# Gate of the first 32 units by Softplus and Erf in groups of three, in place of three Tanh and a Square

## The chip, the cores and the metric

The kernel runs on one core of one Trainium2 chip. Its time is the time on the device, in microseconds (us), of one execution; a number of executions are timed, and their median is given. Engines are named as in the profile: PE is TensorE's matmul, PEld its weight load, DVE is VectorE, ACT is ScalarE, POOL is GpSimd, SP is SyncE, which here issues most transfers.

## The reference

A small attention in two steps, then a feed-forward block with a gate. The gate is h * erf(softplus(h)).

```python
def sm_attn(qq, kk, vv):
    s = scale * np.matmul(qq, kk.transpose(0, 1, 3, 2))
    s = s - np.max(s, axis=-1, keepdims=True)
    a = np.exp(s)
    a = a / (np.sum(a, axis=-1, keepdims=True) + 1e-09)
    return np.matmul(a, vv)
p_packed = sm_attn(p, k, v)
out = sm_attn(q, p_packed, p_packed)
...
h = x @ w_in
sp = np.maximum(h, 0.0) + np.log1p(np.exp(-np.abs(h)))
g = h * erf(sp)
return (g @ w_out).astype(np.float32)
```

There are 8 batches of 8 heads, 576 positions and 64 numbers to a head; 32 packed queries p for each head. x is the attention's result, 4608 rows of 512; w_in is 512 x 2048 and w_out 2048 x 512. Both weights come as 64-bit floats.

## The kernel before

**Units.** The feed-forward part is cut into units. A unit (b, c, i) takes batch b, half c of its 576 positions (288 columns) and block i of eight blocks of 256 hidden features. `h_block` makes h for a unit in two PSUM tiles of 128 x 288 (12 matmuls, L264), copies them to one SBUF tile hs of 128 x 576 (L267, two passes on ACT, times 0.5) and applies the gate. `o_block` multiplies the gated tile with w_out and adds into four PSUM banks (L308). There are 128 units in a list. The first 32 are batches 0 and 1: first blocks 0 to 3 for the four pairs (b, c), 16 units, then blocks 4 to 7. This way only half the weights are needed at the start. The other 96 take batches 2 to 7 in turn, all eight blocks of one half after the other.

**The gate.** erf(softplus(h)) is not computed as written: it is approximated by three Tanh and a Square on ACT, with two weighted sums on DVE (L270 to L275), and a last product with hs. All these functions lie in the one activation table that is loaded at the start (L71), with Exp. In the first 12 units ("whole") the gated tile g goes to PE as it is in fp32. From unit 12 on it is split into a high and a low part (gh, gl, L286 and L287), and three matmuls in the faster fp32r type take the place of the fp32 one. h is always made from split operands.

**Attention.** `attention(b)` is a generator of 12 stages: loads of p and k, of v, of q; scores in two halves (L165); Exp of the first softmax (L174); transposes; the packed values pt (L198, L203); scores of the second step in two halves (L212, L215); Exp of the second softmax (L222); last its normalisation and the split of the result into a2h and a2l (L232, L233). `w_prime(b, j)` multiplies pt with a block of 512 features of w_in (L243) and splits the product (wph, wpl; L245, L246); this takes the place of forming x. h of batch b needs both a2 and these products.

**Weights.** A tile of the weights comes by DMA into a staging buffer (two of them, besides six places lent early by other tiles) and is turned from 64-bit to 32-bit by one pass on ACT (L87) and three on DVE (L88 to L90). 32 such tiles are needed; the last 24 are spread over the units by a plan. `split_w_out` splits w_out's tiles, from unit 14 on for the first half (L103, L104).

**What sets the order.** Loops emit the work unit by unit: h of unit n, then the planned items of unit n (`do(plan.pop(n, []))`: weights, stages of attention, w_prime, splits), then the out product of unit n - 3 (LAG). That order is a priority. A scheduler then gives each engine a fixed queue from it, by its own model of time. An engine works its queue in order, so an instruction that waits holds up all behind it on the same engine. ATT1 = (0, 2) spreads the 12 stages of batch 1's attention over the plan of units 0 to 2; batch 1's first unit is unit 8. Batch 2's stages lie at units 14 to 30, its first unit is unit 32. Pools: hs, t0 and t1 have three buffers each, gh and gl two each.

Of the kernel before, what the change touches and what calls it, by code (L numbers as in the profile page):

```python
# [8 lines left out]
F32 = mybir.dt.float32  # L9
F32R = mybir.dt.float32r  # L10
U32 = mybir.dt.uint32
I64 = mybir.dt.int64
AF = mybir.ActivationFunctionType
ALU = mybir.AluOpType
# [10 lines left out]
F64_SCALE = 2.0 ** -112  # L25
# [3 lines left out]
def tile_pack_attention_moe(ctx: ExitStack, tc: tile.TileContext, qT, kT, v, pT, w_in, w_out, outT):  # L29
    nc = tc.nc  # L30
    P = 128
    B, _, NC, S = qT.shape
    DFF = w_in.shape[1]
    DM = w_out.shape[1]
    HT = S // 2
# [3 lines left out]
    NBLK = DFF // (2 * P)  # L39
# [3 lines left out]
    NK = 32  # L43
    SCALE = 0.125
    LAG = 3
    NB0 = 2
    TURNS = (0, NBLK // 2, NBLK)
    WHOLE = 12
    SPLIT = 14
    WI_AT = (-1, 1)  # L50
    ATT1 = (0, 2)
    ATT2 = 14
    CONV = 2

# [7 lines left out]
    tpool = ctx.enter_context(tc.tile_pool(name="tmp", bufs=3))  # L62
# [5 lines left out]
    bias = cpool.tile([P, 4], F32, name="bias")  # L68
# [7 lines left out]
    def load_f32(dst, src, name, pool=None, tag="wst"):  # L76

        if src.dtype == F32:
            nc.sync.dma_start(dst, src)
            return  # L80
        n = src.shape[1]
        st = (pool or spool).tile([P, n], I64, name=name, tag=tag)
        nc.sync.dma_start(st[:], src)
        words = st[:].bitcast(U32).rearrange("p (n two) -> p n two", two=2)
        low, high = words[:, :, 0], words[:, :, 1]
        bits = dst.bitcast(U32)
        nc.scalar.activation(dst, high.bitcast(F32), AF.Abs, scale=F64_SCALE)  # L87
        nc.vector.tensor_scalar(bits, bits, 3, None, op0=ALU.logical_shift_left)  # L88
        nc.vector.scalar_tensor_tensor(bits, high, 0x80000000, bits, op0=ALU.bitwise_and, op1=ALU.bitwise_or)  # L89
        nc.vector.scalar_tensor_tensor(bits, low, 29, bits, op0=ALU.logical_shift_right, op1=ALU.bitwise_or)  # L90
# [9 lines left out]
    def split_w_out(f):  # L100
        hi = opool.tile([P, DM], F32R, name=f"woh{f}", tag="wo")
        lo = opool.tile([P, DM], F32R, name=f"wol{f}", tag="wo")
        nc.scalar.copy(hi[:], wo[f][:])  # L103
        nc.vector.tensor_tensor(lo[:], wo[f][:], hi[:], op=ALU.subtract)  # L104
        wo_hi[f], wo_lo[f] = hi, lo

    a2 = {}
    pt = {}
# [5 lines left out]
    def attention(b, roomy=False):  # L114
# [30 lines left out]
        k = [chunk(f"k{c}") for c in range(NC)]  # L145
# [5 lines left out]
        for j in range(NCH):  # L151
            n = min(P, S - j * P)
# [7 lines left out]
        a1 = apool.tile([P, 2, S], F32, name=f"a1_{b}", tag="big")  # L160
# [8 lines left out]
        m = apool.tile([P, 2], F32, name=f"m{b}", tag="m")  # L169
        nc.vector.tensor_reduce(m[:], a1[:], axis=AX.X, op=ALU.max)  # L170
        nc.vector.tensor_scalar(m[:], m[:], -SCALE, None, op0=ALU.mult)
        sm = apool.tile([P, 2], F32, name=f"sm{b}", tag="sm")
        for r in range(2):
            nc.scalar.activation(a1[:, r, :], a1[:, r, :], AF.Exp, bias=m[:, r:r + 1], scale=SCALE,  # L174
                                 accum_out=sm[:, r:r + 1])
        nc.vector.tensor_scalar(sm[:], sm[:], 1e-9, None, op0=ALU.add)
        nc.vector.reciprocal(sm[:], sm[:])
        for r in range(2):
# [15 lines left out]
        for j in range(NCH):  # L194
            n = min(P, S - j * P)
# [11 lines left out]
        ta = apool.tile([P, 2, S], F32, name=f"ta{b}", tag="big")  # L207
# [11 lines left out]
        wide = mx[:].unsqueeze(2).to_broadcast([P, 4 * nb, NK])  # L219
        nc.vector.tensor_reduce(mx[:], blocks, axis=AX.X, op=ALU.max)  # L220
        nc.vector.tensor_tensor(blocks, blocks, wide, op=ALU.subtract)
        nc.scalar.activation(ta[:], ta[:], AF.Exp, scale=SCALE)  # L222
        yield
        nc.vector.tensor_reduce(mx[:], blocks, axis=AX.X, op=ALU.add)
        nc.vector.tensor_scalar(mx[:], mx[:], 1e-9, None, op0=ALU.add)
# [21 lines left out]
        wp[b, j] = (hi, lo)  # L247

    gs = {}

    def h_block(b, c, i, whole):


        hs = tpool.tile([P, 2, HT], F32, name=f"hs{b}_{c}_{i}", tag="hs")
        for k in range(2):
            f = (2 * i + k) * P
            j, fo = f // FB, f % FB
            whi, wlo = wp[b, j]
            ps = ps_h.tile([P, 512], F32, name=f"h{b}_{c}_{i}_{k}", tag="ps_h")
            n = 0  # L260
            ahi, alo = a2[b]
            for r in range(2):
                for w, a in ((whi, ahi), (whi, alo), (wlo, ahi)):
                    nc.tensor.matmul(ps[:, 0:HT], w[:, r, fo:fo + P], a[:, r, c * HT:(c + 1) * HT],  # L264
                                     start=(n == 0), stop=(n == 5))
                    n += 1
            nc.scalar.mul(hs[:, k, :], ps[:, 0:HT], 0.5)  # L267
        t = tpool.tile([P, 2, HT], F32, name=f"t{b}_{c}_{i}", tag="t0")
        u = tpool.tile([P, 2, HT], F32, name=f"u{b}_{c}_{i}", tag="t1")
        nc.scalar.activation(t[:], hs[:], AF.Tanh, bias=bias[:, 0:1], scale=2.0 * T_SCALE)  # L270
        nc.scalar.activation(t[:], t[:], AF.Square, bias=bias[:, 1:2], scale=Q_SCALE)  # L271
        nc.scalar.activation(u[:], t[:], AF.Tanh, bias=bias[:, 2:3], scale=U_SCALE)  # L272
        nc.vector.scalar_tensor_tensor(t[:], t[:], 0.5 * A2, hs[:], op0=ALU.mult, op1=ALU.add)  # L273
        nc.vector.scalar_tensor_tensor(t[:], u[:], 0.5 * A1, t[:], op0=ALU.mult, op1=ALU.add)  # L274
        nc.scalar.activation(t[:], t[:], AF.Tanh, bias=bias[:, 3:4], scale=2.0 * A_SCALE)  # L275
        if whole:
            k = len(wholes) % 2
            wholes.append(i)
            g = tpool.tile([P, 2, HT], F32, name=f"g{b}_{c}_{i}", tag=("gh", "gl")[k], bufs=2)
            nc.vector.scalar_tensor_tensor(g[:], t[:], 1.0, hs[:], op0=ALU.add, op1=ALU.mult)  # L280
            gs[b, c, i] = (g,)
            return
        nc.vector.scalar_tensor_tensor(hs[:], t[:], 1.0, hs[:], op0=ALU.add, op1=ALU.mult)  # L283
        ghi = tpool.tile([P, 2, HT], F32R, name=f"gh{b}_{c}_{i}", tag="gh", bufs=2)
        glo = tpool.tile([P, 2, HT], F32R, name=f"gl{b}_{c}_{i}", tag="gl", bufs=2)
        nc.vector.tensor_copy(ghi[:], hs[:])  # L286
        nc.vector.tensor_tensor(glo[:], hs[:], ghi[:], op=ALU.subtract)  # L287
        gs[b, c, i] = (ghi, glo)

    wholes = []  # L290
    acc = {}
# [2 lines left out]
    def o_block(b, c, i, first, last):  # L294

        g = gs.pop((b, c, i))
        t0 = b * S + c * HT
        if first:
            acc[b, c] = []
            for d in range(NDM):  # L300
                po = ps_o.tile([P, 512], F32, name=f"o{b}_{c}_{i}_{d}", tag=f"ps_o{d}")
                acc[b, c].append(po)
        for d in range(NDM):
            for k in range(2):
                f = 2 * i + k
                terms = [(wo, g[0])] if len(g) == 1 else [(wo_hi, g[0]), (wo_hi, g[1]), (wo_lo, g[0])]
                for n, (w, gg) in enumerate(terms):
                    nc.tensor.matmul(acc[b, c][d][:, 0:HT], w[f][:, d * P:(d + 1) * P], gg[:, k, :],  # L308
                                     start=(first and k == 0 and n == 0),
                                     stop=(last and k == 1 and n == len(terms) - 1))  # L310
        if not last:
            return
        for d in range(NDM):
            ob = tpool.tile([P, HT], F32, name=f"ob{b}_{c}_{i}_{d}", tag="ob", bufs=NDM)
            nc.scalar.copy(ob[:], acc[b, c][d][:, 0:HT])
            where = outT[d * P:(d + 1) * P, t0:t0 + HT]
            if (b, c) in begun:
                nc.gpsimd.dma_start(where, ob[:], accum_op=ALU.add)
            else:
                nc.sync.dma_start(where, ob[:])  # L320
        begun.add((b, c))
# [4 lines left out]
    units = [(b, c, i, i == i0, i == i1 - 1) for b, c, i0, i1 in segs for i in range(i0, i1)]  # L326
# [50 lines left out]
    for k, (b, j) in enumerate(uses):  # L377
        if b not in ready:
            plan_attention(b)
        n = ready[b]  # L380
# [13 lines left out]
    def do(items):  # L394
        for it in items:
            if it[0] == "att":
                b = it[1]
                if b not in gens:
                    gens[b] = attention(b)
                next(gens[b])  # L400
            elif it[0] == "sp":
                split_w_out(it[1])
            elif it[0] in ("wi", "wo"):
                conversions[0] += 1
                slot = {}
                if 2 < conversions[0] <= 2 + len(EARLY):
                    slot = dict(pool=wpool, tag=EARLY[conversions[0] - 3])
                if it[0] == "wi":
                    load_w_in(it[1], it[2], **slot)
                else:  # L410
                    load_w_out(it[1], **slot)
            elif it[1:] == (0, 0):
                with tc.high_priority():
                    w_prime(0, 0)
            else:
                w_prime(it[1], it[2])
# [9 lines left out]
    for _ in range(STAGES - 3):  # L426
        next(first)
    do(early[4:])
    for n in range(len(units) + LAG):
        if n < len(units):  # L430
            h_block(*units[n][:3], n < WHOLE)
            do(plan.pop(n, []))
        if n >= LAG:
            o_block(*units[n - LAG])


# [36 lines left out]
```

## Time and profile before

| | us |
|---|---|
| median of 3 runs | 792.11 |
| lowest, highest | 791.83, 792.88 |
| the profiled execution, its own time | 789.89 |
| its span in the profile | 788.1 |

The profile follows one execution on the chip. Busy time is given for each engine, and idle time of an engine is put down to what ended it. A group of instructions has a line, an engine, an operation, its operands, the count, the busy time, the mean duration of one in ns and the idle time just before them. The page cuts the span into 40 slices of 19.7 us and gives the busy share of each in tenths; of these rows the ones of DVE, of ACT and of the clock that PE was granted (9 stands for nine tenths or more):

```profile
DVE  3887898977689678867887769767886769766664
ACT  3357778988689878887687868778687867878784
PEclk8568999999999999999999999999999999999999
```

The first 250 us are the first 13 digits: weights are turned there, two batches pass through attention, and the first 32 units are worked.

### The profile page before, as it was taken

How to read it: one execution, taken by the hardware profiler on the slowest of the kernel's cores; microseconds unless marked ns; L12 is line 12 of the kernel's file. 1: busy time of each engine (PE TensorE's matmuls, PEld its weight loads, DVE VectorE, ACT ScalarE, POOL GpSimd, SP SyncE). 2: the span in 40 equal slices, each digit the busy share in tenths (PEclk: the TensorE clock that was granted, in tenths of full speed). 3: DMA queues.
4: the chain of work that ended last, by engine and by line, in shares of the span. 5: the costliest groups of instructions: out<-in, count | busy, mean ns of one | idle time of the engine just before them, and what ended most of it. 6: DMA issues, size and time to landing. Idle time of an engine off the chain costs nothing.

```text
span 788.1 us, 15219 instructions
## 1 busy us (share of the span) xinstructions
PE 744.6 (94%) x6256; PEld 664.1 (84%) x6256; DVE 599.7 (76%) x916; ACT 597.6 (76%) x1011; POOL 15.1 (2%) x22
## 2 busy tenths in 40 slices
PE   3549988999999999999999999999999999999998
PEld 2228756899998898899799998889888998899998
DVE  3887898977689678867887769767886769766664
ACT  3357778988689878887687868778687867878784
POOL 0000000000111100000000000000000000000000
PEclk8568999999999999999999999999999999999999
DMA  8834735002542422013200222002300210000000
GB/s 306 291 110 149 243 116 162 31 17 67 107 88 31 83 76 89 1 39 98 80 32 1 83 81 72 13 1 80 132 32 1 79 47 1 31 2 31 1 31 31
DMA packets 31813, 58.39 MB, mean 74 GB/s; under 512 B 3584, under 2 KB 14848, under 8 KB 31744
## 3 DMA queue, kind: packets, MB, share of 16 engines
q1 hardware_dynamic: 29440, 55.06, 21.5%
q0 software_dynamic: 2304, 2.36, 2.6%
q8 instruction: 49, 0.80, 0.4%
q14 instruction: 20, 0.16, 0.1%
HBM read 45.61 MB, written 11.80 MB: 73 GB/s over the span
## 4 chain that ended last, share of the span: by engine, by line
PE 82%; DVE 7%; DMA 6%; ACT 3%; issue 1%; SPq 0%; ACTq 0%
PE o L308 50%; PE h L264 24%; PE wp L243 4%; DMA wi<-w_in 4%; DMA wos<-w_out 2%; PE p L198 2%; PE s L212 1%; PE s L165 1%; PE t L186 1%; DVE w_in_sb L89 1%; ACT t L270 1%; DVE wo L89 1%; ACT wo L87 1%; DVE w_in_sb L90 1%; DVE g L280 0%
## 5 line engine op out<-in xcount | busy, mean ns | idle before, releaser
L308 PE MATMUL o<-gl,woh 128*128 128x288 f32 x928 | 273.3, 295 | 0.0
L308 PE MATMUL o<-gh,woh 128*128 128x288 f32 x928 | 273.1, 300 | 0.0
L308 PE MATMUL o<-gh,wol 128*128 128x288 f32 x928 | 272.9, 295 | 0.0
L308 PEld LDWEIGHTS o<-gh,woh 128*128 128x128 f32 x928 | 172.1, 187 | 25.5 <-DVE t L273 8.9
L308 PEld LDWEIGHTS o<-gl,woh 128*128 128x128 f32 x928 | 174.3, 188 | 1.8 <-issue 1.3
L308 PEld LDWEIGHTS o<-gh,wol 128*128 128x128 f32 x928 | 174.6, 188 | 1.5 <-issue 1.3
L267 ACT ACTIVATE hs<-h 128x288 f32<-128x288 f32 x256 | 103.2, 412 | 95.4 <-PE h L264 94.6
L264 PE MATMUL h<-a2h,wph 128*128 128x288 f32 x512 | 155.2, 304 | 10.6 <-ACT wph L245 5.9
L264 PE MATMUL h<-a2l,wph 128*128 128x288 f32 x512 | 152.7, 298 | 1.8 <-DVE a2l L233 1.8
L264 PE MATMUL h<-a2h,wpl 128*128 128x288 f32 x512 | 152.6, 298 | 0.0
L283 DVE SCALAR_TENSOR_TENSOR hs<-t,hs 128x576 f32<-128x576 f32 x116 | 87.7, 756 | 72.5 <-ACT t L275 72.5
L275 ACT ACTIVATE t<-t,bias 128x576 f32<-128x576 f32 x128 | 98.8, 772 | 25.3 <-DVE t L274 25.0
L264 PEld LDWEIGHTS h<-a2h,wph 128*128 128x128 f32 x512 | 97.2, 190 | 22.3 <-ACT wph L245 6.8
L273 DVE SCALAR_TENSOR_TENSOR t<-t,hs 128x576 f32<-128x576 f32 x128 | 95.9, 750 | 20.1 <-ACT u L272 19.8
L270 ACT ACTIVATE t<-hs,bias 128x576 f32<-128x576 f32 x128 | 99.6, 778 | 2.9
L271 ACT ACTIVATE t<-t,bias 128x576 f32<-128x576 f32 x128 | 99.3, 775 | 2.3
L264 PEld LDWEIGHTS h<-a2l,wph 128*128 128x128 f32 x512 | 97.4, 190 | 4.3 <-DVE a2l L233 2.8
L272 ACT ACTIVATE u<-t,bias 128x576 f32<-128x576 f32 x128 | 99.3, 776 | 1.8
L264 PEld LDWEIGHTS h<-a2h,wpl 128*128 128x128 f32 x512 | 97.3, 190 | 1.9 <-issue 1.9
L274 DVE SCALAR_TENSOR_TENSOR t<-u,t 128x576 f32<-128x576 f32 x128 | 96.3, 752 | 1.6
L287 DVE TENSOR_TENSOR gl<-hs,gh 128x576 fp32r<-128x576 f32 x116 | 87.3, 753 | 1.5
L286 DVE CAST gh<-hs 128x576 fp32r<-128x576 f32 x116 | 52.9, 456 | 35.0 <-PE o L308 33.8
(60 smaller groups left out, 637.3 us busy)
## 6 DMA issues: line engine op xcount, KB each, us to landing
k<-kT SPq DMA_DIRECT2D x32, 288.0 KB, 4.3
q<-qT SPq DMA_DIRECT2D x32, 288.0 KB, 4.3
outT<-ob SPq DMA_DIRECT2D x64, 144.0 KB, 1.8
wi<-w_in SPq DMA_DIRECT2D x16, 512.0 KB, 6.0
v<-v SPq DMA_DIRECT2D x32, 256.0 KB, 3.6
wos<-w_out SPq DMA_DIRECT2D x16, 512.0 KB, 3.6
outT<-ob POOLq DMA_DIRECT2D x16, 144.0 KB, 3.7
v<-v SPq DMA_DIRECT2D x8, 128.0 KB, 4.2
```

Of the source, the lines that this page charges most:

```text
L264: nc.tensor.matmul(ps[:, 0:HT], w[:, r, fo:fo + P], a[:, r, c * HT:(c + 1) * HT], start=(n == 0), stop=(n == 5))
L267: nc.scalar.mul(hs[:, k, :], ps[:, 0:HT], 0.5)
L270: nc.scalar.activation(t[:], hs[:], AF.Tanh, bias=bias[:, 0:1], scale=2.0 * T_SCALE)
L271: nc.scalar.activation(t[:], t[:], AF.Square, bias=bias[:, 1:2], scale=Q_SCALE)
L272: nc.scalar.activation(u[:], t[:], AF.Tanh, bias=bias[:, 2:3], scale=U_SCALE)
L273: nc.vector.scalar_tensor_tensor(t[:], t[:], 0.5 * A2, hs[:], op0=ALU.mult, op1=ALU.add)
L274: nc.vector.scalar_tensor_tensor(t[:], u[:], 0.5 * A1, t[:], op0=ALU.mult, op1=ALU.add)
L275: nc.scalar.activation(t[:], t[:], AF.Tanh, bias=bias[:, 3:4], scale=2.0 * A_SCALE)
L283: nc.vector.scalar_tensor_tensor(hs[:], t[:], 1.0, hs[:], op0=ALU.add, op1=ALU.mult)
L286: nc.vector.tensor_copy(ghi[:], hs[:])
L287: nc.vector.tensor_tensor(glo[:], hs[:], ghi[:], op=ALU.subtract)
L308: nc.tensor.matmul(acc[b, c][d][:, 0:HT], w[f][:, d * P:(d + 1) * P], gg[:, k, :], start=(first and k == 0 and n == 0), stop=(last and k = ...
```

## The change

In the first 32 units (GROUPED) the gate is now computed as written: Softplus, Erf and a product. Softplus and Erf are done for three units at a time: three Softplus, then three Erf, then the products (and splits) of the three. 32 units make ten groups of three and one of two. A chain of dependencies without a wait (`in_turn`) fixes the order of Softplus, Erf and attention's Exp on ACT while units 0 to 31 are emitted. hs is no longer halved in these units, and its buffers alternate between the tags hs and t1 from group to group. Out products run 5 units behind while n < 32 (LAG_G), then 3 as before. The stages of batch 1's attention are spread over units 1 to 6. The pass on ACT that turns weights is a multiplication in place of Abs. From unit 32 on the gate is as it was.

```diff
+    G = 3
+    GROUPED = 4 * NBLK
+    LAG_G = 5
...
-    ATT1 = (0, 2)
+    ATT1 = (1, 6)
...
-        nc.scalar.activation(dst, high.bitcast(F32), AF.Abs, scale=F64_SCALE)
+        nc.scalar.mul(dst, high.bitcast(F32), F64_SCALE)
...
+    functions = []
+    grouping = [True]
+
+    def in_turn(ins):
+
+        if grouping[0] and functions:
+            tc.add_manual_dep(ins.ins, functions[-1], mybir.DependencyInfo(
+                mybir.DependencyClass.NoSync, mybir.DependencyReason.DATA), reason="table")
+        functions.append(ins.ins.name)
...
-            nc.scalar.activation(a1[:, r, :], a1[:, r, :], AF.Exp, bias=m[:, r:r + 1], scale=SCALE,
-                                 accum_out=sm[:, r:r + 1])
+            in_turn(nc.scalar.activation(a1[:, r, :], a1[:, r, :], AF.Exp, bias=m[:, r:r + 1], scale=SCALE,
+                                         accum_out=sm[:, r:r + 1]))
...
-        nc.scalar.activation(ta[:], ta[:], AF.Exp, scale=SCALE)
+        in_turn(nc.scalar.activation(ta[:], ta[:], AF.Exp, scale=SCALE))
...
+    group = []
...
+    def gate_group():
+
+        ts = []
+        for hs, b, c, i, whole in group:
+            t = tpool.tile([P, 2, HT], F32, name=f"t{b}_{c}_{i}", tag="t0")
+            in_turn(nc.scalar.activation(t[:], hs[:], AF.Softplus))
+            ts.append(t)
+        for t in ts:
+            in_turn(nc.scalar.activation(t[:], t[:], AF.Erf))
+        for t, (hs, b, c, i, whole) in zip(ts, group):
+            if whole:
+                nc.vector.tensor_tensor(whole_g(b, c, i)[:], t[:], hs[:], op=ALU.mult)
+            else:
+                nc.vector.tensor_tensor(hs[:], t[:], hs[:], op=ALU.mult)
+                split_g(hs, b, c, i)
+        group.clear()
...
+        grouped = n < GROUPED
+        hs = tpool.tile([P, 2, HT], F32, name=f"hs{b}_{c}_{i}", tag="t1" if grouped and n // G % 2 else "hs")
...
-            nc.scalar.mul(hs[:, k, :], ps[:, 0:HT], 0.5)
+            if grouped:
+                nc.scalar.copy(hs[:, k, :], ps[:, 0:HT])
+            else:
+                nc.scalar.mul(hs[:, k, :], ps[:, 0:HT], 0.5)
+        if grouped:
+            group.append((hs, b, c, i, whole))
+            if len(group) == G or n == GROUPED - 1:
+                gate_group()
+            return
...
+    behind = 0
     for n in range(len(units) + LAG):
         if n < len(units):
-            h_block(*units[n][:3], n < WHOLE)
+            grouping[0] = n < GROUPED
+            h_block(*units[n][:3], n < WHOLE, n)
             do(plan.pop(n, []))
-        if n >= LAG:
-            o_block(*units[n - LAG])
+        while behind <= n - (LAG_G if n < GROUPED else LAG):
+            o_block(*units[behind])
+            behind += 1
```

`whole_g` and `split_g` hold the lines that made g, or gh and gl, in `h_block` before.

More of the change, by code (lines that the diff above doesn't have):

```diff
@@ L249, in tile_pack_attention_moe, with split_g, whole_g, h_block @@
     gs = {}
-    def h_block(b, c, i, whole):
-        hs = tpool.tile([P, 2, HT], F32, name=f"hs{b}_{c}_{i}", tag="hs")
+    group = []
+    def split_g(hs, b, c, i):
+        ghi = tpool.tile([P, 2, HT], F32R, name=f"gh{b}_{c}_{i}", tag="gh", bufs=2)
+        glo = tpool.tile([P, 2, HT], F32R, name=f"gl{b}_{c}_{i}", tag="gl", bufs=2)
+        nc.vector.tensor_copy(ghi[:], hs[:])
+        nc.vector.tensor_tensor(glo[:], hs[:], ghi[:], op=ALU.subtract)
+        gs[b, c, i] = (ghi, glo)
+    def whole_g(b, c, i):
+        k = len(wholes) % 2
+        wholes.append(i)
+        g = tpool.tile([P, 2, HT], F32, name=f"g{b}_{c}_{i}", tag=("gh", "gl")[k], bufs=2)
+        gs[b, c, i] = (g,)
+        return g
+    def gate_group():
[13 more added lines that the diff above has]
+        group.clear()
+    def h_block(b, c, i, whole, n):
+        grouped = n < GROUPED
+        hs = tpool.tile([P, 2, HT], F32, name=f"hs{b}_{c}_{i}", tag="t1" if grouped and n // G % 2 else "hs")
         for k in range(2):
@@ L259, in h_block @@
             ps = ps_h.tile([P, 512], F32, name=f"h{b}_{c}_{i}_{k}", tag="ps_h")
-            n = 0
+            m = 0
             ahi, alo = a2[b]
@@ L264, in h_block @@
                     nc.tensor.matmul(ps[:, 0:HT], w[:, r, fo:fo + P], a[:, r, c * HT:(c + 1) * HT],
-                                     start=(n == 0), stop=(n == 5))
-                    n += 1
-            nc.scalar.mul(hs[:, k, :], ps[:, 0:HT], 0.5)
+                                     start=(m == 0), stop=(m == 5))
+                    m += 1
+            if grouped:
[7 more added lines that the diff above has]
+            return
         t = tpool.tile([P, 2, HT], F32, name=f"t{b}_{c}_{i}", tag="t0")
@@ L276, in h_block @@
         if whole:
[L277 to L281, printed above, removed]
+            nc.vector.scalar_tensor_tensor(whole_g(b, c, i)[:], t[:], 1.0, hs[:], op0=ALU.add, op1=ALU.mult)
             return
         nc.vector.scalar_tensor_tensor(hs[:], t[:], 1.0, hs[:], op0=ALU.add, op1=ALU.mult)
[L284 to L288, printed above, removed]
+        split_g(hs, b, c, i)
     wholes = []
```

## The prediction

> **What bounds the kernel now.** I read the page first (engines, then the 40 slices), then who TensorE (PE) waited for, then the stretches between 80 and 140 us, then the lines of time around the longest waits.
>
> ```profile
> span 788.1 us, 15219 instructions
> PE 744.6 (94%) x6256; PEld 664.1 (84%) x6256; DVE 599.7 (76%) x916; ACT 597.6 (76%) x1011; POOL 15.1 (2%) x22
> ...
> PE   3549988999999999999999999999999999999998
> ```
>
> PE is the bound from about the seventh slice on. Its busy time is modelled, so I use only its waits and the order of its groups. Who PE waited for between 46 and 160 us (us in total, times, longest):
>
> ```profile
> PE h L264 <- ACT wph L245: 5.9, 1, 5.9
> PE wp L243 <- DVE wpl L246: 2.3, 2, 1.8
> PE wp L243 <- DVE w_in_sb L90: 1.9, 2, 1.4
> PE h L264 <- DVE a2l L233: 1.8, 1, 1.8
> PE o L308 <- DVE g L280: 1.8, 2, 1.2
> PE t L186 <- DVE wpl L246: 1.0, 1, 1.0
> PE h L264 <- ACT hs L267: 0.5, 2, 0.3
> ```
>
> Together 15.2 us. The same view from 160 us to the end has its heading and no row. How far the units with the changed gate reach is seen from the product at L273, one for each unit, between 46 and 245 us (DVE busy, count, clock, DMA share, GB/s):
>
> ```profile
> 46.00:245.00 199.00, 23.29 (x31) 0.96 0.38 108
> ```
>
> So units 0 to 31 fill 46 to about 245 us, and the 96 units behind them, where PE never waits, keep their code. Whatever the change saves on ACT and DVE, it can win at most these 15.2 us and what the waits hide. The stretches (busy us of PE, PEld, DVE, ACT, POOL, then granted clock, DMA share, GB/s):
>
> ```profile
> 80.00:100.00 20.00, 19.91 (x131) 14.18 (x130) 17.12 (x29) 16.28 (x30) 0.00 (x0) 1.00 0.74 251
> 100.00:120.00 20.00, 16.49 (x85) 10.80 (x84) 20.00 (x30) 14.00 (x21) 0.00 (x0) 0.91 0.32 99
> 120.00:140.00 20.00, 17.42 (x114) 12.61 (x114) 16.15 (x27) 17.98 (x34) 0.00 (x0) 1.00 0.46 146
> 140.00:160.00 20.00, 20.00 (x126) 16.73 (x125) 18.41 (x28) 18.71 (x36) 0.00 (x0) 1.00 0.09 31
> ```
>
> From 100 to 120 DVE is busy all the time and PE starves. What it starves of is attention of batch 1, which unit 8 needs (lines of time; start, us):
>
> ```profile
> 55.35 0.76 ACT L174 ACTIVATE a<-a,m 128x576 f32<-128x576 f32 x1
> ...
> 57.72 0.99 ACT L245 CAST wph<-wp 128x1024 fp32r<-128x1024 f32 x1
> ```
>
> ```profile
> 116.38 1.34 DVE L233 TENSOR_TENSOR a2l<-tb,a2h 128x1152 fp32r<-128x1152 f32 x1
> ```
>
> ```profile
> 46.34 0.61 PE L264 MATMUL h<-a2l,wph 128*128 128x288 f32 x1 [1.81 <-DVE a2l L233]
> ...
> 78.57 4.04 PE L308 MATMUL o<-g,wo 128*128 128x288 f32 x16
> ...
> 106.94 5.84 PE L308 MATMUL o<-g,wo 128*128 128x288 f32 x16
> ...
> 115.58 4.15 PE L308 MATMUL o<-g,wo 128*128 128x288 f32 x16 [1.17 <-DVE g L280]
> 119.35 0.64 PE L264 MATMUL h<-a2h,wph 128*128 128x288 f32 x2
> ```
>
> Batch 1's first Exp starts at 55.35, its last split ends at 117.7, and h of unit 8 starts at 119.35. Ahead of it PE has done the out products of units 0 to 7, the last two at 106.94 and 115.58.
>
> **The change, part by part.** The groups that carry prices (busy us, mean ns; idle before):
>
> ```profile
> L267 ACT ACTIVATE hs<-h 128x288 f32<-128x288 f32 x256 | 103.2, 412 | 95.4 <-PE h L264 94.6
> L270 ACT ACTIVATE t<-hs,bias 128x576 f32<-128x576 f32 x128 | 99.6, 778 | 2.9
> L275 ACT ACTIVATE t<-t,bias 128x576 f32<-128x576 f32 x128 | 98.8, 772 | 25.3 <-DVE t L274 25.0
> L273 DVE SCALAR_TENSOR_TENSOR t<-t,hs 128x576 f32<-128x576 f32 x128 | 95.9, 750 | 20.1 <-ACT u L272 19.8
> L274 DVE SCALAR_TENSOR_TENSOR t<-u,t 128x576 f32<-128x576 f32 x128 | 96.3, 752 | 1.6
> L280 DVE SCALAR_TENSOR_TENSOR g<-t,hs 128x576 f32<-128x576 f32 x12 | 9.0, 749 | 0.2 <-ACT t L275 0.2
> L222 ACT ACTIVATE ta<-ta 128x1152 f32<-128x1152 f32 x8 | 9.3, 1166 | 9.0 <-DVE ta L221 8.9
> L246 DVE TENSOR_TENSOR wpl<-wp,wph 128x1024 fp32r<-128x1024 f32 x32 | 38.9, 1216 | 6.1 <-ACT wph L245 5.0
> L138 ACT COPY a<-s 128x576 f32<-128x576 f32 x14 | 8.8, 626 | 1.8 <-PE s L165 1.7
> L71 ACT ACT_TABLE_LOAD x1 | 1.3, 1283 | 0.7 <-PEq L465 0.7
> ```
>
> 1. *DVE.* L273 and L274 go, and the product at L280/L283 becomes a plain product of the same size (taken at 750). Per unit 0.750+0.752 = 1.50 us less, 48 us over 32 units.
>
> 2. *ACT functions.* Four passes of about 775 become two without a bias tile. The trace has neither Softplus nor Erf. The passes without a bias tile are 626 (a copy of 576) and 1166 (Exp of 1152); from 412 at 288 to 1166 at 1152 a line gives 0.66 at 576. I take 0.67, ends 0.626 and 0.778. The edits from mul 0.5 to copy and from Abs to mul are one pass for one pass: nothing, also in their waits.
>
> 3. *Table loads.* The trace has one, 1283 ns. Taking it that Softplus, Erf and Exp each need their own table (the diff strings them together with the reason "table"), 32 units are 11 groups with 2 loads each, the two Exp places of batch 1 and the two of batch 2 fall between groups and add 4, the return to Exp and Tanh adds 1: 27 more. I take 1.28 us each, as the row nearest to it is the thing itself; its ends are 0 where it runs while ACT waits for data anyway, and twice the row, 2.57, if the engine also empties around it. So ACT for three whole units was 6 x 0.412 + 12 x 0.775 = 11.8 us and becomes 6 x 0.412 + 6 x 0.67 + 2 x 1.28 = 9.1 (11.6 by the upper end). PE needs about three times 1.6 + 4.04 = 17 us for the same three units (h: 12 matmuls in 1.60 us; out product: the row at 78.57):
>
> ```profile
> 144.19 1.60 PE h L264 x12
> ```
>
> So ACT stays under PE in the steady part. The Trainium skill, "ScalarE: Activation LUTs", section "What ACT_TABLE_LOAD costs", puts a switch at 1283 ns plus a drain of about 1380 ns, 2.66 us in all; the trace agrees with the first part and cannot show the second, its only load standing ahead of all work. By that page three units would take 6 x 0.412 + 6 x 0.67 + 2 x 2.66 = 11.8 us, an estimate, so ACT would win nothing.
>
> 4. *Lag 5.* Between h of the last unit of a group and the first out product of that group PE has three h and three out products, 14 to 17 us. The gate chain of a group after that h is an eviction, one Softplus, a load, an Erf and one DVE product: 0.41+0.67+1.28+0.67+0.75 = 3.8 us, plus what stands ahead in the queues. I count no wait in the steady part. The two buffers each of gh and gl make the third unit of a group wait for its first one's out product, which is done a whole unit ahead of the third one's: nothing, as long as PE runs. At unit 32 three out products are caught up, the same work as before.
>
> 5. *The wait that is added.* Erf of units 6 and 7 stands behind Softplus of unit 8 on ACT, and unit 8 needs batch 1. So out products 6 and 7, which now fill PE until 119.35, can run only after it. Queued behind: PE has nothing but six out products ahead of h of unit 8.
>
> 6. *Batch 1 is moved.* Its stages go from units 0 to 2 to units 1 to 6, so its loads go behind the second block of w_in and the first two of w_out on SP's queue (a gain for those, a loss for k; both hidden, as its scores run while PE waits for that w_in block's product anyway). Its first Exp now stands behind Erf of unit 2. Unit 2 needs the split whose cast starts at 57.72; with batch 1's Exps and a tanh gone from ahead of it I take it 2 us earlier, then split, h, eviction, Softplus, load, three Erf and load: 1.0+1.2+1.6+0.4+0.7+1.3+2.0+1.3 = 9.5, so Exp at about 65 instead of 55.35.
>
> *The sum.* Let T be the end of batch 1's last split (before: 117.7). From 46.34 to 119.35 are 73.0 us, with waits of 15.2 less 1.8 (a2l, at its start) and less 2.6 that come after 119.35 (1.4 of w_in_sb, 0.5 of hs, 0.6 of g): 10.8. The out product at 106.94 took 5.84 where 4.04 is usual, so 1.8 more are hidden. Work: 73.0-10.8-1.8 = 60.4, less out products 6 and 7 (8.1): 52.3. PE would be through with it at 98.6; then it waits until T. Allowing 1.0 for later waits in place of 2.6, the change is (T-98.6+1.0) - (10.8+1.8+2.6) = T - 112.8. For T: the chain from first Exp to last split took 62.4 us in a DVE queue that is nearly full. Removed from that queue are 8 units x 2.25 = 18 us, put in 6 units x 0.75 = 4.5: 13.5 less. 65+62.4-13.5 = 113.9. A queue no longer full also costs each chain step less; I take 5 us for that, about a third of the removed work, by choice. T = 109, change **-3.8 us**. The ends: T at or below 98.6 gives -14.2; T with no relief at all, 127, gives +15. The profiled execution ran 789.89 us for a span of 788.1; 786.1 after it. The median of the runs shown is 2.2 us higher, so 788.3 on that scale.
>
> **The rivals.**
> - *A, forecast, 0.40*: as above, 781 to 790.5.
> - *B, the waits nearly vanish, 0.20*: batch 1 is ready by 101.5. For: only short DVE ops stand between its steps then. Against: its first Exp is 10 us later. 792.1-14 to -11: 778 to 781.
> - *C, the new wait takes the place, 0.19*: out products 6 and 7 held behind batch 1 (part 5) cost 8 us of PE, and DVE's relief is used up by weight conversions that move forward. It decides from T = 114.4 on; at T = 120, +7: 799, range 793.7 to 802.
> - *D, the switches cost twice the row, 0.08*: 27 x 1.28 = 35 us more on ACT, which from 120 to 160 us is busy 36.7 of 40. ACT then wins nothing, and two switches and the Erf ahead lengthen the chain by some 4 us: T about 117, +4, 796. More loads than 27 (the order not kept) would look the same. The Trainium skill, "ScalarE: Activation LUTs", section "What ACT_TABLE_LOAD costs", states a rule of this kind, a drain with every switch.
> - *E, no difference, 0.13*: the start is paced by the weights (transfer, ACT, DVE, two staging buffers), as the chain of waits has it:
>
> ```profile
> 84.89 3.50 DMA wos<-w_out
> 90.44 3.80 DMA wos<-w_out
> 118.96 3.92 DMA wi<-w_in
> ```
>
> Then relief on DVE changes little: 790.5 to 793.7.
>
> **How the numbers follow.** A measurement of this kernel tells about 0.2% (1.6 us) from no change. Faster: A+B = 0.60; same: E = 0.13; slower: C+D = 0.27. Range 778 to 799: it leaves out the upper part of C, about 0.1, and little below B, and its ends are those that T (the sum) and the load (part 3) give. The likeliest sign's own range is 778 to 790.5.
>
> **What would show it.** Right: DVE under 17 of 20 between 100 and 120 us; 28 loads of about 1.3 us; h of unit 8 before 112; waits of PE up to 138 us near 12 in sum and none behind. Wrong: a wait of PE on a g or on hs after 140 us (part 4), loads with an idle ACT of over 1 us behind them (part 3), h of unit 8 at 119 or later with PE idle before it (part 5), or Exp of batch 1 at 70 or later (part 6).

## The result and the profile after

The changed kernel takes 819.79 us (median of 4 runs, 819.15 to 820.72) against 792.39 before: the ratio is 1.0347, interval 1.0329 to 1.0365. It is 27 us slower, outside the predicted range. The profiled execution ran 820.72 us for a span of 818.9. The page after, engines and three rows of the slices:

```profile
span 818.9 us, 15125 instructions
PE 749.7 (92%) x6256; PEld 664.5 (81%) x6256; DVE 560.9 (68%) x852; ACT 583.0 (71%) x974; POOL 15.0 (2%) x22
...
PE   3359844999999999999999999999999999999998
...
DVE  3886668343438567977697678867797778776664
...
PEclk8569965999999999999999999999999999999999
```

In both kernels PE is at nine tenths or more from the eighth digit to the last but one, though DVE is busy 39 us less than before. The sixth and seventh digits (about 100 to 140 us), which were 8, are now 4: PE idle, and with a lowered clock. The stretches of that time (busy us of PE, PEld, DVE, ACT, POOL; clock, DMA share, GB/s):

```profile
100.00:120.00 20.00, 10.60 (x124) 5.99 (x120) 13.56 (x24) 3.97 (x8) 0.00 (x0) 0.74 0.79 258
120.00:140.00 20.00, 6.88 (x45) 2.91 (x45) 16.21 (x22) 13.22 (x18) 0.00 (x0) 0.57 0.16 53
140.00:160.00 20.00, 19.87 (x111) 13.81 (x112) 6.11 (x9) 15.70 (x27) 0.00 (x0) 0.91 0.09 30
```

From 100 to 120 us DVE is no longer full (13.56 for 20.00), ACT almost idle, and the transfers run at 258 GB/s. None of the compute engines is full. Who PE waited for after 46 us; these rows come to 33.1, and to 38.3 with six smaller ones that are not shown, where it was 15.2:

```profile
PE wp L256 <- DVE wpl L259: 11.2, 2, 10.8
PE s L225 <- DVE ta L228: 4.2, 1, 4.2
PE o L354 <- DVE g L290: 4.2, 2, 2.4
PE h L310 <- ACT wph L258: 4.0, 1, 4.0
PE h L310 <- ACT a2h L245: 3.5, 1, 3.5
PE h L310 <- ACT hs L314: 3.0, 2, 2.0
PE h L310 <- DVE a2l L246: 3.0, 1, 3.0
```

So 23 of the 31 us between the two spans are waits of PE after 46 us. 2.4 more are waits before it (27.4 for 25.0). What is left, 5 us, is PE working longer on the same 6256 matmuls (749.7 for 744.6 us busy), at a lower clock. The product with w_in behind the longest wait takes 1.96 us, where the one at 105.86 took 1.09 in the kernel before:

```profile
127.19 1.96 PE L256 MATMUL wp<-w_in_sb,pt 64*32 64x512 f32 x16 [10.81 <-DVE wpl L259]
```

What PE waits for is batch 1. Lines of time of ACT, up to its first Exp:

```profile
66.04 0.62 ACT L151 COPY a<-s 128x576 f32<-128x576 f32 x1
...
73.23 0.67 ACT L90 ACTIVATE wo<-wos 128x512 f32<-128x512 f32 x1 [4.82 <-DMA wos<-w_out]
73.81 0.62 ACT L151 COPY a<-s 128x576 f32<-128x576 f32 x1
...
77.95 1.28 ACT L187 ACT_TABLE_LOAD   x1 [0.33 <-DVE m L184]
79.25 0.78 ACT L187 ACTIVATE a<-a,m 128x576 f32<-128x576 f32 x1
```

and up to its second:

```profile
108.19 0.66 ACT L90 ACTIVATE w_in_sb<-wi 128x512 f32<-128x512 f32 x1 [5.38 <-DMA wi<-w_in]
110.94 0.66 ACT L90 ACTIVATE w_in_sb<-wi 128x512 f32<-128x512 f32 x1 [2.09 <-DMA wi<-w_in]
114.29 0.68 ACT L90 ACTIVATE wo<-wos 128x512 f32<-128x512 f32 x1 [2.69 <-DMA wos<-w_out]
119.28 0.66 ACT L90 ACTIVATE wo<-wos 128x512 f32<-128x512 f32 x1 [4.30 <-DMA wos<-w_out]
119.95 1.28 ACT L235 ACT_TABLE_LOAD   x1
121.25 1.16 ACT L235 ACTIVATE ta<-ta 128x1152 f32<-128x1152 f32 x1
```

The first Exp comes at 79.25 in place of 55.35, and each step stands in ACT's queue behind passes over weights whose transfers have not landed. On DVE, the data of the second Exp was ready at 118.56; ACT was held by the weights until 119.94. The longest wait of PE, 10.8 us, ends the same way: the split that it waits for needs a cast, and the product to be cast was there at 116.4, but the cast stood in ACT's queue behind the last of these weights, the Exp, two Softplus and two loads:

```profile
124.88 0.99 ACT L258 CAST wph<-wp 128x1024 fp32r<-128x1024 f32 x1
```

The last split of batch 1:

```profile
133.80 1.35 DVE L246 TENSOR_TENSOR a2l<-tb,a2h 128x1152 fp32r<-128x1152 f32 x1
```

It ends at 135.15 (T of the prediction), 17 us later than before.

### The profile page after: what moved, and what is told of

The parts are those of the page before. It is cut to its first block, busy times and chain, and to the rows that moved or that the text cites. A ratio compares the mean times of both kernels' runs of the same rounds, so it can differ in the third digit from the quotient of the medians.

```text
span 818.9 us, 15125 instructions
## 1 busy us (share of the span) xinstructions
PE 749.7 (92%) x6256; PEld 664.5 (81%) x6256; DVE 560.9 (68%) x852; ACT 583.0 (71%) x974; POOL 15.0 (2%) x22
## 4 chain that ended last, share of the span: by engine, by line
PE 80%; DMA 7%; ACT 6%; DVE 5%; issue 1%; SPq 1%; ACTq 0%
PE o L354 49%; PE h L310 23%; PE wp L256 4%; DMA wi<-w_in 4%; PE p L211 2%; DMA q<-qT 1%; PE s L225 1%; DMA wos<-w_out 1%; PE s L178 1%; PE t L199 1%; DVE wo L92 1%; ACT L287 1%; ACT t L287 1%; ACT w_in_sb L90 1%; ACT t L284 1%
## 5 line engine op out<-in xcount | busy, mean ns | idle before, releaser
L310 PE MATMUL h<-a2h,wph 128*128 128x288 f32 x512 | 157.3, 308 | 20.4 <-ACT a2h L245 13.4
L316 ACT ACTIVATE hs<-h 128x288 f32<-128x288 f32 x192 | 78.2, 412 | 80.4 <-PE h L310 77.3
L333 DVE SCALAR_TENSOR_TENSOR hs<-t,hs 128x576 f32<-128x576 f32 x96 | 72.5, 755 | 60.4 <-ACT t L329 60.4
L329 ACT ACTIVATE t<-t,bias 128x576 f32<-128x576 f32 x96 | 74.0, 771 | 22.9 <-DVE t L328 22.7
L327 DVE SCALAR_TENSOR_TENSOR t<-t,hs 128x576 f32<-128x576 f32 x96 | 71.8, 748 | 13.0 <-ACT u L326 12.8
L324 ACT ACTIVATE t<-hs,bias 128x576 f32<-128x576 f32 x96 | 74.4, 776 | 2.2
L325 ACT ACTIVATE t<-t,bias 128x576 f32<-128x576 f32 x96 | 74.3, 774 | 1.9
L326 ACT ACTIVATE u<-t,bias 128x576 f32<-128x576 f32 x96 | 74.5, 776 | 1.5
L328 DVE SCALAR_TENSOR_TENSOR t<-u,t 128x576 f32<-128x576 f32 x96 | 72.3, 753 | 1.2
```

## The experiments

Three theories. **M**: batch 1's stages were moved late, and PE has nothing to do until it is there. **W**: Erf of units 6 and 7 waits for unit 8, so their out products can't fill the gap. **L**: the table loads. A table of the runs stands at the end of this section; T is the end of batch 1's last split.

**e1: the stages alone.**
```diff
 (before)
-    ATT1 = (0, 2)
+    ATT1 = (1, 6)
```


> The kernel before with one edit: the stages of batch 1's attention spread over units 1 to 6 in place of 0 to 2, gate and lag as before. Theory M (batch 1 was moved late, and PE has nothing to do until it is there): last split of batch 1 at 128 us or later in place of 117.7, time 800 to 812. Theory W (the wait of units 6 and 7 for unit 8 in a group of three): 792 to 795, since no group exists here. Theory L (table loads): 792 to 795.

811.33 us, ratio 1.0248 (1.0211 to 1.0285), with no Softplus, no group and no load in it. First Exp and last split, lines of time of ACT and of DVE:

```profile
79.16 0.76 ACT L174 ACTIVATE a<-a,m 128x576 f32<-128x576 f32 x1
```
```profile
135.11 1.35 DVE L233 TENSOR_TENSOR a2l<-tb,a2h 128x1152 fp32r<-128x1152 f32 x1
```

The same two times as in the changed kernel, to a microsecond or two. M holds and carries 20 of the 27 us (811.33 for 791.2). W and L alone are excluded.

**e2: no loads.**
```diff
 (after)
-            in_turn(nc.scalar.activation(t[:], hs[:], AF.Softplus))
+            in_turn(nc.scalar.activation(t[:], hs[:], AF.Tanh))
...
-            in_turn(nc.scalar.activation(t[:], t[:], AF.Erf))
+            in_turn(nc.scalar.activation(t[:], t[:], AF.Tanh))
```


> The changed kernel with Tanh in place of Softplus and of Erf: same number of passes in the same order, but one table serves all, so 27 loads go. The gate is another function than the reference's. L: 27 x 1.28 = 35 us of ACT go, time 795 to 803. M and W: the loads lie in time in which ACT waits for transfers or PE has work, time 812 to 820.

812.0 us (1.0228 to 1.0294): 27 loads, 34.6 us of ACT, are worth 7 to 8 us of time. This lies at the low end of what M and W expected, and 9 us above what L did: the loads matter, but are not the main part.

**e3: groups cut where the batch changes.**
```diff
 (after; and the tags of hs alternate by a count of groups)
-            if len(group) == G or n == GROUPED - 1:
+            if len(group) == G or n == GROUPED - 1 or units[n + 1][0] != b:
```


> The changed kernel with a group closed where the batch changes (units 6 and 7 by themselves, 8 to 10, 11 to 13, 14 and 15, and so on), so that no Erf waits for the first unit of the next batch; some loads more. W: out products 6 and 7, about 8 us of PE, run before batch 1 is there: 820 - 8 = 812, at most 810. M: batch 1 is as late as before, so the 8 us are all that can come back, 811 to 816. L: more loads, 820 to 823.

813.8 us (1.0247 to 1.0325), 5 to 6 us less than the changed kernel, with two loads more; the two intervals nearly touch. It lies where M expected it and above W's 810. T stays at 136.3. PE starts on the out products of units 6 and 7 at 128.58, in the changed kernel at 144.68: their wait is real and worth up to 6 us while batch 1 is late.

**e4: stages early, Exp free.**
```diff
 (after; both Exp without in_turn)
-    ATT1 = (1, 6)
+    ATT1 = (0, 2)
```


> The changed kernel with the stages of batch 1 at units 0 to 2 again, and attention's Exp left out of the fixed order (Softplus and Erf keep theirs), so that Exp can go ahead as soon as its data is there; some loads more. M: last split of batch 1 at 120 us or earlier in place of 135, time 795 to 805. W: units 6 and 7 still wait for unit 8, so 812 to 820. L: more loads, 820 to 825.

799.88 us (1.0076 to 1.0141). T is 107.4, and 20 us come back, as many as e1 lost. Two things differ here from the changed kernel, the place of the stages and the free Exp; e13 below has the place alone. But Erf of units 6 to 8 is still late, for another reason:

```profile
119.04 0.70 ACT L90 ACTIVATE w_in_sb<-wi 128x512 f32<-128x512 f32 x1 [1.00 <-DMA wi<-w_in]
119.62 0.69 ACT L284 ACTIVATE t<-hs 128x576 f32<-128x576 f32 x1
120.33 1.28 ACT L287 ACT_TABLE_LOAD   x1
121.63 1.83 ACT L287 ACTIVATE t<-t 128x576 f32<-128x576 f32 x3
```

Unit 8's Softplus runs 12 us after its batch is there, behind weights again.

**e5 and e6: e4 with groups cut as in e3; and that without loads as in e2.**

```diff
 (e5: e4, and for e6 besides AF.Tanh twice as in e2)
-            if len(group) == G or n == GROUPED - 1:
+            if len(group) == G or n == GROUPED - 1 or units[n + 1][0] != b:
```


> e4_att02_free with groups also closed where the batch changes. In e4 batch 1's last split ended at 107.4 us, yet the Erf of units 6 and 7 ran at 121.6, behind the Softplus of unit 8, which stood behind weight passes that waited for transfers. W (this wait is what is left of the loss): 8 us of out products come before it, time 792 to 796. Against W: 798 to 802, what is left lies in the loads.

> e5_free_cut with Tanh in place of Softplus and of Erf, so without any load but the first; the gate is another function than the reference's. L: the loads cost what they did in e2_no_loads, 8 us: 8 less than e5_free_cut, 4 us at least. Against L: with batch 1 early they lie where ACT waits anyway, within 2 us of e5_free_cut.

e5: 800.84 us (1.0076 to 1.0118), no less than e4, with two loads more: with batch 1 early, W is worth nothing that shows. e6: 793.2 us (0.9995 to 1.0015), 7.6 less than e5 and equal to before. So the 8 to 9 us that e4 and e5 are slower are nearly all loads. After 46 us PE waits 20.8 us in e5 and 14.7 in e6. The two largest differences are waits for copies on ACT: wph (7.9 and 5.5) and ob (3.1 and 0.3). The first, ACT in e5, then in e6:

```profile
53.82 1.28 ACT L187 ACT_TABLE_LOAD   x1
...
57.60 1.28 ACT L285 ACT_TABLE_LOAD   x1
58.89 0.68 ACT L285 ACTIVATE t<-hs 128x576 f32<-128x576 f32 x1
59.48 0.99 ACT L258 CAST wph<-wp 128x1024 fp32r<-128x1024 f32 x1
```
```profile
57.02 0.67 ACT L285 ACTIVATE t<-hs 128x576 f32<-128x576 f32 x1
57.60 0.99 ACT L258 CAST wph<-wp 128x1024 fp32r<-128x1024 f32 x1
```

Two loads stand ahead of the cast of wph for which PE waits. e6 also shows that the relief bought nothing here: it has the changed kernel's fewer passes, no loads but the first, and T = 102.8, and is as fast as before. The waits of PE after 46 us come to 14.7, where they were 15.2. Those for copies of hs grew from 0.5 to 3.8: such copies stand behind passes over weights that wait for transfers, 3.03 and 4.09 us for two of them. The groups of three and the longer lag stay in e6, so it isn't shown whether the fewer passes would gain without them.

**e7: units 0 to 7 as before, 8 to 31 grouped.**
```diff
 (e4)
+    FIRST_G = 8
...
-        grouped = n < GROUPED
+        grouped = FIRST_G <= n < GROUPED
```


> Units 0 to 7 with the gate of before and lag 3, units 8 to 31 by Softplus and Erf in threes with lag 5; stages of batch 1 at units 0 to 2, Exp outside the fixed order. If the loss lies wholly ahead of unit 8 (M and W): 788 to 794, as ACT and DVE have less to do from unit 8 on but PE hardly waits there. If the grouped gate costs by itself, wherever it stands (L): 796 or more.

796.97 us (1.0033 to 1.007), 4 us over before with 20 loads more, and T = 118.2, as before. The first expectation is missed: the grouped gate costs also behind unit 8. In the waits of PE there are 2.4 us for hs and 1.9 for ob, both copies on ACT.

**e8: the weights' first pass on POOL.**
```diff
 (after)
-        nc.scalar.mul(dst, high.bitcast(F32), F64_SCALE)
+        nc.gpsimd.tensor_scalar(dst, high.bitcast(F32), F64_SCALE, None, op0=ALU.mult)
```


> The changed kernel with the first pass over the weights on POOL in place of ACT. M's mechanism (weight passes that wait for a transfer stand in ACT's queue ahead of batch 1's steps and hold them): ACT no longer waits for transfers, last split of batch 1 at 128 us or earlier, time 800 to 812. Against it (batch 1 is late by its place in the queues alone, or by DVE's passes, which still wait): 815 to 825.

813.05 us (1.0236 to 1.0283), T = 130.3: between the expectations. A pass on POOL is also longer (last section). Some 5 of the 17 us by which T is late go with ACT's waits for transfers; the first Exp is still at 78.33, now behind 6.3 us in which ACT waits for DVE's maximum (m). Weights in ACT's queue are a part of why batch 1 is late. What is left over is more, and lies in the place of its steps on the other queues; how much each queue holds was not measured.

**e9, e10, e11: does the weights' stream hold the kernel before?** The pass on POOL as in e8; three staging buffers in place of two; both.

```diff
 (before; e9 the first, e10 the second, e11 both)
-        nc.scalar.activation(dst, high.bitcast(F32), AF.Abs, scale=F64_SCALE)
+        nc.gpsimd.tensor_scalar(dst, high.bitcast(F32), F64_SCALE, None, op0=ALU.mult)
...
-    spool = ctx.enter_context(tc.tile_pool(name="stage", bufs=2))
+    spool = ctx.enter_context(tc.tile_pool(name="stage", bufs=3))
```

> The kernel before with the first pass over the weights on POOL in place of ACT. e6 had 48 us of DVE and 50 us of ACT less than before and was no faster, so the start is bound by something else. Theory S (weights that wait for a transfer stand in ACT's queue): the wait of PE for wph, 5.9 us, goes or halves, 785 to 790. Rival (the weights' stream is paced by its transfers and two buffers, wherever the pass runs): 791 to 795.

> The kernel before with three staging buffers for the weights in place of two. If the stream is paced by the two buffers: 784 to 790, with the last pass over a weight tile at 135 us or earlier in place of 142. If the passes' places in the queues pace it: 791 to 795.

> The kernel before with both edits, the pass on POOL and three staging buffers. If each takes away a limit of its own: 780 to 787, faster than both kernels and than either edit alone. If they take away the same one: as the better of the two.

None is faster: 793.71 (1.0003 to 1.0029), 793.53 (1.0009 to 1.0038) and 800.76 (1.0089 to 1.013). The first two lie where their rivals expected them, the third above both of its expectations. In e9 PE no longer waits for wph, but 5.1 us for g; in e10 the last weights are there earlier (last pass at 124.6, before at 141.7), yet PE waits 6.0 us for a2h at the start and T is 125.1. In e11, T is 129.6, 12 us later than before. Each takes a wait away and gets another.

**e12: e4 with three staging buffers**, the second edit of the diff above.

> e4_att02_free (the changed kernel, batch 1 at units 0 to 2, Exp outside the fixed order) with three staging buffers. If the staging is what kept the relief of DVE and ACT from being used: under 791, faster than before by more than e10 is against it less 8 us of loads, 783 to 790. If not: 797 to 801 as e4.

796.25 us (1.0035 to 1.007): about 4 less than e4, not the 9 at least that were expected. None of these beats the kernel before.

**e13, e14, e15: start, end, and the fixed order.** e13 is the changed kernel with ATT1 = (0, 2) and the fixed order kept; e14 and e15 are the kernel before with ATT1 = (0, 6) and (1, 2).

```diff
 (e13: after)
-    ATT1 = (1, 6)
+    ATT1 = (0, 2)
 (e14, e15: before)
-    ATT1 = (0, 2)
+    ATT1 = (0, 6)
...
+    ATT1 = (1, 2)
```

> The changed kernel with only the stages of batch 1 put back to units 0 to 2; Exp stays in the fixed order, so both Exps of batch 1 stand ahead of the first Softplus of unit 0. If the fixed order is what asks for the later stages: group 0 has to wait for the second Exp of batch 1 (94 us in e4), PE has six h at most before that, time over 820, 825 to 845. If the order of Exp matters little: 798 to 803 as e4.

> The kernel before with batch 1's stages spread over units 0 to 6: its loads and first scores stay early, the later ones go back. If the late start costs (stage 0 behind the second block of w_in): under 800, 792 to 798. If the late end costs (the last stages behind the weights of units 3 to 6): 803 to 812, as with 1 to 6.

> The kernel before with batch 1's stages at units 1 to 2: start one unit later, end as before. If the late start costs: 803 to 812, first Exp of batch 1 at 75 us or later. If the late end costs: 791 to 797.

e14: 805.88 us (1.014 to 1.0208), first Exp at 73.62. e15: 807.69 us (1.0159 to 1.0216), first Exp at 72.96. Either shift alone costs 14 to 16 us, both together 20: not start or end alone, but each step of batch 1 that falls behind weights and units. Each run lies where one of its two expectations put it, and they name different ends; the first Exp of e15 was expected at 75 or later. e13: 805.25 us (1.0134 to 1.0197), between its two expectations (over 820, and 798 to 803). So in the changed kernel the place of the stages alone is worth 14.5 us. The second Exp then has no Softplus or Erf ahead of it and runs at 84.27 (94.87 in e4), so group 0 can start at 85, and PE waits 21.5 us after 46 us, in place of 38.3 with late stages. The fixed order does not force the late place; it costs 5 us against e4.

Batch 1's times in the runs that move its stages or the weights (the kernel before ran 791.2 to 792.9 us beside them):

| kernel | first Exp, us | T, us | time, us |
|---|---|---|---|
| before | 55.4 | 117.7 | 792.4 |
| after | 79.3 | 135.2 | 819.8 |
| e1 before, ATT1 (1, 6) | 79.2 | 136.5 | 811.3 |
| e14 before, ATT1 (0, 6) | 73.6 | 133.1 | 805.9 |
| e15 before, ATT1 (1, 2) | 73.0 | 132.6 | 807.7 |
| e9 before, pass on POOL | 51.8 | 114.5 | 793.7 |
| e10 before, three buffers | 60.1 | 125.1 | 793.5 |
| e11 before, both | 54.6 | 129.6 | 800.8 |
| e2 after, no loads | 77.6 | 129.0 | 812.0 |
| e3 after, cut | 79.5 | 136.3 | 813.8 |
| e8 after, pass on POOL | 78.3 | 130.3 | 813.1 |
| e13 after, ATT1 (0, 2) | 55.2 | 103.0 | 805.3 |
| e4 after, (0, 2), Exp free | 56.1 | 107.4 | 799.9 |
| e5 e4, cut | 55.1 | 108.6 | 800.8 |
| e6 e5, no loads | 54.7 | 102.8 | 793.2 |

## Why the prediction was wrong

The step that failed is part 6, and with it T. It said of moving batch 1's stages "a gain for those, a loss for k; both hidden", and put its first Exp at 65. The scores, which ran at 37.08 and 43.31 before, ran at 61.12 and 71.36, since their place in the queues was now behind the units and the weights; and the Exp came at 79.25. The loads of k, which the prediction took to be the loss, were not late: SP issued batch 1's last one at about 17 us before and at 18.03 now. The edit alone is 20 us in the kernel before (e1); in the changed kernel, undoing it gives 14.5 (e13), and 20 with Exp free (e4). It was priced by what it waits for, not by what stands ahead of it in the queues.

The second step that failed is in the sum: "13.5 less" for DVE's relief, and 5 more. From first Exp to last split the chain took 55.9 us (79.25 to 135.15) in place of 62.4: 6.5 less, not 18.5. So T = 109 was missed by 14 us in its start and by 12 in its length. The place that DVE won was filled by waiting. From 46 to 140 us ACT waited 29.1 us for weights, before 15.9:

```profile
ACT w_in_sb L90 <- DMA wi<-w_in: 15.1, 6, 5.4
ACT wo L90 <- DMA wos<-w_out: 14.0, 5, 4.8
```
```profile
ACT w_in_sb L87 <- DMA wi<-w_in: 10.5, 6, 3.3
ACT wo L87 <- DMA wos<-w_out: 5.4, 7, 1.7
```

Point by point:
- *The frame of the sum holds only for a late T.* T - 112.8 with the measured T of 135.2 gives +22.4, and PE's waits after 46 us grew by 23.1; it has no term for the waits before 46 us (2.4) and for the lower clock (5). But it takes every wait between 46 us and T as gone, and they don't go: with T = 102.8 it gives 10 us less than before, and e6, which has neither the loads nor the held out products, measured 0.3 more. So an early batch 1 would not have won what the forecast and *rival B* took it to win. (The later waits that it takes off, 1.4, 0.5 and 0.6, make 2.5, not 2.6.)
- *Parts 1 and 2 held* in their sizes: a product on DVE takes 754 and 753 ns, Softplus 686, Erf 675 (taken 750 and 670).
- *Part 3* had the count right, 27 loads at 1283 ns each, but took them as hidden by PE. They are worth 7 to 8 us (e2, and e5 against e6); the first of them stand in ACT's queue ahead of copies for which PE waits. The groups of loads:

```profile
L284 ACT ACT_TABLE_LOAD x11 | 14.1, 1283 | 0.2
L287 ACT ACT_TABLE_LOAD x11 | 14.1, 1283 | 0.2
L187 ACT ACT_TABLE_LOAD x3 | 3.8, 1283 | 0.4 <-DVE m L184 0.3
L235 ACT ACT_TABLE_LOAD x2 | 2.6, 1283 | 0.0
```

- *Part 4 held nearly*: from 145 us on PE waits 2.7 us in all, for q, gl and ob.
- *Part 5* named a real wait, worth up to 6 us (e3), and nothing that shows once batch 1 is early (e5).
- *Rival C* was the right kind of ending, decided from T = 114.4; T was 15 us past the value at which it was priced. *Rival D* fell: a switch costs its row and no more (below).
- *Rival E* said that relief on DVE changes little. e6 bears that out, with the groups and the lag in place. That its cause is the staging of the weights was tried (e9 to e11) and not shown: what paces the first 140 us of the kernel before stays open. A third buffer and a free ACT each moved the wait and not the end.
- *The signs.* DVE under 17 of 20 between 100 and 120 us came (13.56) and was to mean a gain; DVE was waiting. Against it stood the first Exp at 79.25 and h of unit 8 at 132.69, with PE idle before it.

The loss adds up as: 20 us by the stages' place (e1), 8 by the loads, and about 0 by all the rest, the wait of units 6 and 7 being part of what the late batch costs. The parts overlap: without the loads, T too falls from 135.2 to 129.0.

## What to carry to other kernels

Where engines work fixed queues in order, price a moved step by what will stand ahead of it on every queue that it crosses, above all instructions that wait for transfers; not by the work that would hide it. Time taken off an engine that is full is only worth something if the next thing in its queue is ready: look first at which waits in the queue are for transfers. A sum that takes the old waits as gone has to say what else could fill them. Grouping passes to have fewer table loads has to count the first groups, where copies that PE needs stand behind the loads, apart from the steady part.

## What the runs showed of the hardware

- A table switch between passes cost its load and nothing visible beside it. In the changed kernel, ACT around one group:

```profile
85.04 0.70 ACT L284 ACTIVATE t<-hs 128x576 f32<-128x576 f32 x1
85.76 1.28 ACT L287 ACT_TABLE_LOAD   x1
87.05 1.83 ACT L287 ACTIVATE t<-t 128x576 f32<-128x576 f32 x3
```

The load starts 0.02 us after the pass ends and the next pass 0.01 us after the load. The Trainium skill, "ScalarE: Activation LUTs", section "What ACT_TABLE_LOAD costs", adds a drain of about 1380 ns to each switch; the trace differs, and the measurement decides. All that a switch loses besides is the overlap of passes that follow each other (three Erf of 675 ns each take 1.83 us together).
- The pass over a weight tile, 128 x 512, takes 1.65 us on POOL (0.67 on ACT), and DVE's next pass over it grew to 498 ns for w_in's tiles (425 in the changed kernel; groups of e8). No run shows why it grew:

```profile
L90 POOL TENSOR_SCALAR w_in_sb<-wi 128x512 f32<-128x512 f32 x16 | 25.9, 1626 | 46.9 <-DMA wi<-w_in 46.9
L91 DVE TENSOR_SCALAR w_in_sb<-w_in_sb 128x512 uint32<-128x512 uint32 x16 | 8.0, 498 | 13.6 <-POOL w_in_sb L90 13.6
```
- From 120 to 140 us PE was busy 6.88 of 20 us, and its granted clock was 0.57; from 140 to 160 it was busy 19.87, with 0.91. What work PE had there ran slower (1.96 for 1.09 us); 5 us of the 31 between the spans are not waits of PE.
